# Reading the moving operand of the float32r products in an interleaved column order, with blocks of 496 and 512 columns

## The chip, the cores and the metric

The kernel runs on one core of a Trainium2 chip. The metric is the device time of one execution in microseconds. Before the change it is 2344.78 us, the median of 3 runs (2344.65 to 2344.81).

## The reference

Attention over channels, followed by two feed-forward layers, for B = 2 batches of N = 6016 tokens with C = 256 channels:

```
qn = q / (norm(q, axis=1) + 1e-6);  kn = k / (norm(k, axis=1) + 1e-6)
s  = kn.transpose(0, 2, 1) @ qn / tau            # 256 x 256 per batch
a  = softmax(s)                                  # by rows
x  = (v @ a).reshape(B * N, C)
h  = x @ w_in;   g = h - tanh(h);   x = g @ w_out        # 256 -> 2048 -> 256
out = (sigmoid(x @ w_gate) * (x @ w_val)) @ w_out2       # 256 -> 1536 -> 256
```

## The kernel before

A first stage reads q and k of batch 0, forms the 256x256 scores and their softmax, and multiplies the softmax into w_in (`aw_chunk`, L285), so that h comes straight from v: `aw = a @ w_in`. The same for batch 1 runs in the background, between the blocks' products.

The tokens are then taken in 24 blocks, 12 for each batch, of 500, 504 or 512 tokens (`blocks`, L55 to L70: ten of 500, one of 512 and one of 504 in each batch). Tokens are columns: v and out lie in memory as channels by tokens, and each tile of a block has 128 partitions and one column per token. A block goes through four products, each in 128x128 stationary tiles of weights with the block's columns as the moving operand:

- H (`emit_H`, L324 and L326): h = aw^T v, 16 tiles f of 128 features.
- `emit_E` (L334 to L342): g = h - tanh(h) on ScalarE (ACT) and VectorE (DVE).
- X (`emit_X`, L370, L371, L373): x2 = w_out^T g, summed over the 16 tiles f into two PSUM tiles.
- GV (`emit_GV`, L405, L406, L408): gate and value of x2, 12 tiles m; `emit_S` multiplies sigmoid(gate) by value.
- O (`emit_O`, L437): out = w_out2^T p, summed over m into two PSUM tiles; `emit_out` copies and stores them.

Every float32 operand is split into a high part, rounded to float32r, and the low rest, also float32r. A product is then three: high by high, high by low, low by high. So H has 6 matmuls for each f, X 6 for each f, GV 12 for each m and O 6 for each m. That is 96 + 96 + 144 + 72 = 408 matmuls per block. For block 0, and the first 4 tiles f of block 1 (`XF`), X is done in plain float32 (L365) from one unsplit operand instead. A plain float32 product is issued as two matmul instructions, as are the scores of the first stage (L562, L509).

The order of the work is written out by hand: one loop over steps T with 16 steps per block. In a step stand E of tile f-1, the split and X of tile f-2, H of tile f, and GV and O of some tile m of the block before, which the tables `GV0`, `OFF1`, `OFFS` and `OFFL` place. TensorE (PE) runs it in that order. H and GV write into four rotating PSUM tiles (`psw`), so PE cannot run further ahead than ACT and DVE empty these.

Of the kernel before, what the change touches and what calls it, by code (L numbers as in the profile page):

```python
# [26 lines left out]
def kernel(  # L27
# [14 lines left out]
    B, N, C = q.shape  # L42
# [7 lines left out]
    TB = 4 * P  # L50
    MM = nc.tensor.matmul
    NW = 64


    WB = 500  # L55
    nb = -(-N // TB)
    widths = [WB] * nb
    rest, i = N - WB * nb, nb // 2
    assert 0 <= rest <= nb * (TB - WB)
    while rest:  # L60
        x = min(rest, TB - WB)
        widths[i] += x
        rest -= x
        i = (i + 1) % nb
    blocks = []
    for b in range(B):
        t = 0
# [29 lines left out]
    def psw(name, shape=(P, 512)):  # L97
        return ps_w.tile(list(shape), F32, tag="w", name=name)
# [12 lines left out]
    aw_hi = [wp.tile([P, NK, 2 * P], F32R, name=f"awh{i}") for i in range(N1 // 2)]  # L111

    win = [wp.tile([P, NK, 2 * P], F32, tag=f"awl{i}", name=f"win{i}") for i in range(N1 // 2)]
    aw_lo = {}
# [188 lines left out]
    def split_v(p):  # L303
# [8 lines left out]
            out=lo[:, :, :n], in0=vt, in1=h[:, :, :n].bitcast(F32), op=ALU.subtract  # L312
        )

    hps, g_t, ghl = {}, {}, {}

    def emit_H(p, f):
        n = blocks[p][2]
        h, lo = vT[p]
        o = psw(f"h{p}_{f}")  # L320
        i, fs = f // 2, slice((f % 2) * P, (f % 2 + 1) * P)
        for x in (h, lo):
            for kk in range(2):
                MM(o[:, :n], aw_hi[i][:, kk, fs], x[:, kk, :n], start=x is h and kk == 0, stop=False)  # L324
        for kk in range(2):
            MM(o[:, :n], aw_lo[i][:, kk, fs], h[:, kk, :n], start=False, stop=kk == 1)  # L326
        hps[p, f] = o

    def emit_E(p, f):
# [26 lines left out]
    def emit_X(p, f):  # L356
        n = blocks[p][2]
        if f == 0:
            xps[p] = [ps_x.tile([P, 512], F32, tag=f"x{d}", name=f"x{d}_{p}") for d in range(2)]
        i, a = f // 2, f % 2  # L360
        ds = [slice(d * P, (d + 1) * P) for d in range(2)]
        if p == 0 or p == 1 and f < XF:
            g = g_t.pop((p, f))
            for d in range(2):
                MM(xps[p][d][:, :n], w1_f[i][:, a, ds[d]], g, start=f == 0, stop=f == N1 - 1)  # L365
            return
        gh, gl = ghl.pop((p, f))
        for d in range(2):
            o = xps[p][d][:, :n]
            MM(o, w1_hi[i][:, a, ds[d]], gh, start=f == 0, stop=False)  # L370
            MM(o, w1_lo[i][:, a, ds[d]], gh, start=False, stop=False)  # L371
        for d in range(2):
            MM(xps[p][d][:, :n], w1_hi[i][:, a, ds[d]], gl, start=False, stop=f == N1 - 1)  # L373

    x2 = {}
# [19 lines left out]
    gvps, p_t, phl = {}, {}, {}  # L395

    def emit_GV(p, m):
        n = blocks[p][2]
        h, lo = x2[p]
        ms = slice((m % 2) * P, (m % 2 + 1) * P)  # L400
        res = []
        for nm, wht, wlt in (("ga", wg_hi, wg_lo), ("va", wv_hi, wv_lo)):
            o = psw(f"{nm}{p}_{m}")
            for d in range(2):
                MM(o[:, :n], wht[m // 2][:, d, ms], h[d][:, :n], start=d == 0, stop=False)  # L405
                MM(o[:, :n], wlt[m // 2][:, d, ms], h[d][:, :n], start=False, stop=False)  # L406
            for d in range(2):
                MM(o[:, :n], wht[m // 2][:, d, ms], lo[d][:, :n], start=False, stop=d == 1)  # L408
            res.append(o[:, :n])
        gvps[p, m] = res  # L410

# [13 lines left out]
    def emit_O(p, m):  # L425
        n = blocks[p][2]
        if m == 0:
            ops[p] = [ps_o.tile([P, TB], F32, tag=f"o{d}", name=f"o{d}_{p}") for d in range(NK)]
        ph, pl = phl.pop((p, m))
        i, a = m // 2, m % 2  # L430
        ds = [slice(d * P, (d + 1) * P) for d in range(NK)]
        last = p == NB - 1 and m == N2 - 1
        for d, w, x in ((0, w2_hi, ph), (0, w2_lo, ph), (1, w2_hi, ph), *(
            ((0, w2_hi, pl), (1, w2_lo, ph), (1, w2_hi, pl)) if last else
            ((1, w2_lo, ph), (0, w2_hi, pl), (1, w2_hi, pl))
        )):
            MM(ops[p][d][:, :n], w[i][:, a, ds[d]], x, start=m == 0 and w is w2_hi and x is ph,  # L437
               stop=m == N2 - 1 and x is pl)
# [35 lines left out]
    while len(e_of) < NT:  # L474
        for home in ("x2h", "x2l", *(f"rr{i}" for i in range(6))):
            j = len(e_of)
            n = min(2 if home[0] == "x" else 1, NT - j)
# [52 lines left out]
    ms = tc.manual_schedule()  # L530
# [182 lines left out]
    for n in range(3 * N2 // 2):  # L713
        i, w = divmod(n, 3)
# [3 lines left out]
    for j in range(NT):  # L718
        t = 54 + 2 * j
# [36 lines left out]
    for T in range(-4, (NB + 1) * N1 + 18):  # L756
# [14 lines left out]
        for u in mg:  # L771
            emit_GV(*u)
# [3 lines left out]
        if e0 and first:  # L776
            emit_H(*e0)
# [7 lines left out]
        if e2:  # L785
            emit_X(*e2)
            if e2[1] == N1 - 1:
                emit_x2(e2[0])
        for u in mo:
            emit_O(*u)  # L790
# [9 lines left out]
        if e0 and not first:  # L800
            emit_H(*e0)
# [39 lines left out]
```

## Time and profile before

| | |
|---|---|
| time, median of 3 runs | 2344.78 us |
| span of the profiled execution | 2342.6 us |
| PE busy | 2330.5 us (99%) |
| PE weight loads busy | 1932.8 us (83%) |
| DVE busy | 1799.2 us (77%) |
| ACT busy | 1575.5 us (67%) |
| granted TensorE clock | 1.00 from 5 us to the end |

The profiled execution's span is 2.2 us below the median time, since launch and end of the program lie outside it. A busy time is the union of an engine's instructions. The duration of a matmul in the profile reaches from its first column to its modelled end, so consecutive matmuls overlap: what one costs PE is the distance between two starts, not its duration.

### The profile page before, as it was taken

The page shows a single profiled execution, that of the slowest core. Times are in us where ns is not written, and L with a number is a line of the kernel's source. Part 1 is how long each engine was busy: PE and PEld are TensorE (multiplying, and loading weights), DVE is VectorE, ACT ScalarE, POOL GpSimd, SP SyncE. Part 2 cuts the span into 40 slices and gives each one's busy share as a digit, 9 for nine tenths or more (in the row PEclk, how much of TensorE's full clock was granted, in tenths as well). Part 3 has the DMA queues.
Part 4 walks back from the last instruction along what each step waited for, and adds up shares of the span by engine and source line. Part 5 has one row for each costly group of instructions (what it writes and reads, how often), then busy time and mean ns, then how long its engine had stood idle before and what let it go on. Part 6 is the DMA issues. An engine that isn't in the chain of part 4 may idle for free.

```text
span 2342.6 us, 28855 instructions
## 1 busy us (share of the span) xinstructions
PE 2330.5 (99%) x10338; PEld 1932.8 (83%) x10338; DVE 1799.2 (77%) x2791; ACT 1575.5 (67%) x2777; POOL 67.2 (3%) x53
## 2 busy tenths in 40 slices
PE   9999999999999999999999999999999999999999
PEld 7778788888888888888888888888888888888887
DVE  7999877787878777777777777777777777777773
ACT  6677666776767667766676666666666666666663
POOL 0000000111111110000000000000000000000000
PEclk9999999999999999999999999999999999999999
DMA  9742001101101100000000000000000000000000
GB/s 353 225 132 90 27 1 50 33 26 50 32 28 45 32 27 18 1 23 32 18 18 14 6 18 1 18 18 1 18 18 1 18 18 1 18 1 18 10 1 18
DMA packets 54000, 86.54 MB, mean 37 GB/s; under 512 B 4960, under 2 KB 34144, under 8 KB 53856
## 3 DMA queue, kind: packets, MB, share of 16 engines
q1 hardware_dynamic: 53280, 83.91, 11.1%
q8 instruction: 81, 1.33, 0.2%
q10 hardware_dynamic: 576, 0.79, 0.1%
q14 instruction: 63, 0.52, 0.1%
HBM read 69.73 MB, written 14.94 MB: 36 GB/s over the span
## 4 chain that ended last, share of the span: by engine, by line
PE 90%; DVE 7%; ACT 1%; issue 1%; DMA 0%; ACTq 0%; DVEq 0%; SPq 0%
PE o L437 16%; PE h L324 14%; PE h L326 7%; PE x L373 7%; PE x L370 7%; PE x L371 7%; PE ga L405 5%; PE ga L406 5%; PE va L405 5%; PE va L406 5%; PE ga L408 5%; PE va L408 5%; DVE accb L573 1%; DVE w L341 1%; DVE w L342 1%
## 5 line engine op out<-in xcount | busy, mean ns | idle before, releaser
L339 DVE SCALAR_TENSOR_TENSOR w<-u,h 128x500 f32<-128x500 f32 (+2 forms) x384 | 259.3, 675 | 327.0 <-ACT t L335 326.8
L334 ACT ACTIVATE u<-h 128x500 f32<-128x500 f32 (+2 forms) x384 | 223.7, 583 | 248.0 <-PE h L326 245.5
L342 DVE COPY_PREDICATED w<-m,t 128x500 f32<-128x500 uint16 (+2 forms) x384 | 306.2, 797 | 39.9 <-ACT sr L679 0.5
L337 ACT ACTIVATE s<-u,cb 128x500 f32<-128x500 f32 (+2 forms) x384 | 274.5, 715 | 0.7 <-DVE w L341 0.6
L338 ACT ACTIVATE m<-u,ct 128x500 bf16<-128x500 f32 (+2 forms) x384 | 272.8, 710 | 0.0
L340 DVE TENSOR_TENSOR t<-h,t 128x500 f32<-128x500 f32 (+2 forms) x384 | 258.2, 672 | 0.0
L341 DVE SCALAR_TENSOR_TENSOR w<-s,w 128x500 f32<-128x500 f32 (+2 forms) x384 | 257.3, 670 | 0.0
L324 PE MATMUL h<-vTh,awh 128*128 128x500 f32 (+2 forms) x768 | 243.9, 399 | 0.0
L324 PE MATMUL h<-vTl,awh 128*128 128x500 f32 (+2 forms) x768 | 235.4, 387 | 0.9 <-DVE vTl L311 0.9
L326 PE MATMUL h<-vTh,awl 128*128 128x500 f32 (+2 forms) x768 | 235.5, 388 | 0.0
L335 ACT ACTIVATE t<-h 128x500 f32<-128x500 f32 (+2 forms) x384 | 223.6, 582 | 1.7 <-PE x L365 1.0
L405 PE MATMUL ga<-x2h,wgh 128*128 128x500 f32 (+2 forms) x552 | 213.6, 387 | 0.0
L406 PE MATMUL va<-x2h,wvl 128*128 128x500 f32 (+2 forms) x552 | 213.6, 387 | 0.0
L406 PE MATMUL ga<-x2h,wgl 128*128 128x500 f32 (+2 forms) x552 | 213.6, 387 | 0.0
L405 PE MATMUL va<-x2h,wvh 128*128 128x500 f32 (+2 forms) x552 | 213.4, 387 | 0.0
L417 DVE TENSOR_TENSOR sg<-va,sg 128x500 f32<-128x500 f32 (+2 forms) x288 | 192.3, 668 | 20.9 <-PE va L408 20.9
L416 ACT ACTIVATE sg<-ga 128x500 f32<-128x500 f32 (+2 forms) x288 | 169.2, 587 | 15.7 <-PE ga L408 12.8
L408 PE MATMUL ga<-x2l,wgh 128*128 128x500 f32 (+2 forms) x576 | 176.1, 387 | 0.0
L408 PE MATMUL va<-x2l,wvh 128*128 128x500 f32 (+2 forms) x576 | 176.0, 387 | 0.0
L324 PEld LDWEIGHTS h<-vTh,awh 128*128 128x128 f32 x768 | 143.6, 188 | 34.5 <-issue 7.1
L324 PEld LDWEIGHTS h<-vTl,awh 128*128 128x128 f32 x768 | 144.4, 188 | 30.6 <-DVE vTl L311 1.4
L326 PEld LDWEIGHTS h<-vTh,awl 128*128 128x128 f32 x768 | 144.2, 188 | 28.9
(361 smaller groups left out, 4449.8 us busy)
## 6 DMA issues: line engine op xcount, KB each, us to landing
v<-in_v_dram SPq DMA_DIRECT2D x20, 500.0 KB, 4.2
out_dram<-ob SPq DMA_DIRECT2D x19, 500.0 KB, 3.2
sr<-in_q_dram SPq DMA_DIRECT2D x47, 128.0 KB, 2.1
sr<-in_k_dram SPq DMA_DIRECT2D x47, 128.0 KB, 2.2
raw<-in_q_dram SPq DMA_DIRECT2D x13, 384.0 KB, 8.1
raw<-in_k_dram SPq DMA_DIRECT2D x12, 384.0 KB, 8.2
st_wi<-in_moe_w_in_dram SPq DMA_DIRECT2D x8, 512.0 KB, 7.0
st_w<-in_moe_w_out_dram SPq DMA_DIRECT2D x8, 512.0 KB, 4.8
```

What stands on the lines that cost most here:

```text
L324: MM(o[:, :n], aw_hi[i][:, kk, fs], x[:, kk, :n], start=x is h and kk == 0, stop=False)
L326: MM(o[:, :n], aw_lo[i][:, kk, fs], h[:, kk, :n], start=False, stop=kk == 1)
L337: nc.scalar.activation(s, u, AF.Square, bias=cb)
L338: nc.scalar.activation(m, u, AF.Relu, bias=ct2)
L339: nc.vector.scalar_tensor_tensor(out=w, in0=u, scalar=C2, in1=hp, op0=ALU.mult, op1=ALU.mult)
L340: nc.vector.tensor_tensor(out=t, in0=hp, in1=t, op=ALU.subtract)
L341: nc.vector.scalar_tensor_tensor(out=w, in0=s, scalar=CG, in1=w, op0=ALU.add, op1=ALU.mult)
L342: nc.vector.copy_predicated(w, m.bitcast(U16), t)
L405: MM(o[:, :n], wht[m // 2][:, d, ms], h[d][:, :n], start=d == 0, stop=False)
L406: MM(o[:, :n], wlt[m // 2][:, d, ms], h[d][:, :n], start=False, stop=False)
L408: MM(o[:, :n], wht[m // 2][:, d, ms], lo[d][:, :n], start=False, stop=d == 1)
L437: MM(ops[p][d][:, :n], w[i][:, a, ds[d]], x, start=m == 0 and w is w2_hi and x is ph, stop=m == N2 - 1 and x is pl)
```

## The change

Three things change; the sequence of instructions on every engine and queue stays the same, one for one.

1. Each moving operand of H, X, GV and O in float32r is read through a view, `turned`, that takes the columns of each group of 16 in the order 0, 8, 1, 9, 2, 10, and so on to 7, 15. For blocks 0 and 1 (`PB = 2`) the group is 8 columns and the order is 0, 4, 1, 5, 2, 6, 3, 7. The output is written in plain order, so each product permutes the block's columns. Four such products in a row give back the first order for groups of 16, and three do for groups of 8; in blocks 0 and 1 X is read plainly, so there H, GV and O are the three.
2. The widths of the blocks must be multiples of 16. In each batch they become eight of 496 and four of 512 columns. The number of blocks, of matmuls and of columns in all is as before.
3. ACT and DVE read and write their tiles plainly, as before, in the new widths.

```
-    WB = 500
+    QB = 16
+    assert N % QB == 0
     nb = -(-N // TB)
+    WB = N // nb // QB * QB
     widths = [WB] * nb
     rest, i = N - WB * nb, nb // 2
     while rest:
-        x = min(rest, TB - WB)
-        widths[i] += x
-        rest -= x
+        widths[i] += QB
+        rest -= QB
         i = (i + 1) % nb
...
+    PB = 2
+
+    def turned(p, x):
+        return x.rearrange("p (a t i) -> p a i t", t=2, i=4 if p < PB else QB // 2)
...
-                MM(o[:, :n], aw_hi[i][:, kk, fs], x[:, kk, :n], start=x is h and kk == 0, stop=False)
+                MM(o[:, :n], aw_hi[i][:, kk, fs], turned(p, x[:, kk, :n]), start=x is h and kk == 0, stop=False)
...
-        gh, gl = ghl.pop((p, f))
+        gh, gl = (x if p < PB else turned(p, x) for x in ghl.pop((p, f)))
...
-        h, lo = x2[p]
+        h, lo = ([turned(p, x[:, :n]) for x in y] for y in x2[p])
...
-        ph, pl = phl.pop((p, m))
+        ph, pl = (turned(p, x) for x in phl.pop((p, m)))
```

## Rows read from the trace of the kernel before

**Rows 1.** The page, busy time (share of the span) and instructions by engine

```profile
PE 2330.5 (99%) x10338; PEld 1932.8 (83%) x10338; DVE 1799.2 (77%) x2791; ACT 1575.5 (67%) x2777; POOL 67.2 (3%) x53
PEclk9999999999999999999999999999999999999999
```

**Rows 2.** Waits, total us, times, longest: PE's two longest, then DVE's and ACT's

```profile
PE kq L562 <- DMA raw<-in_k_dram: 2.5, 2, 1.4
PE va L406 <- DVE wvl L150: 1.3, 1, 1.3
...
DVE w L339 <- ACT t L335: 326.8, 322, 3.4
ACT u L334 <- PE h L326: 245.5, 177, 3.1
```

**Rows 3.** Windows by block; the fourth row is all from block 3 on

```profile
core 0: us, PE busy (x) PEld busy (x) DVE busy (x) ACT busy (x) POOL busy (x), PEclk, DMA share, GB/s
60.50:140.10 79.60, 79.60 (x311) 58.24 (x309) 76.45 (x133) 52.02 (x91) 0.00 (x0) 1.00 0.63 193
140.10:238.30 98.20, 96.46 (x406) 75.66 (x405) 93.86 (x159) 72.14 (x128) 0.00 (x0) 1.00 0.33 105
238.30:339.70 101.40, 99.51 (x440) 82.12 (x438) 77.53 (x125) 66.11 (x119) 0.00 (x0) 1.00 0.05 16
339.70:2338.70 1999.00, 1998.73 (x8927) 1668.66 (x8925) 1502.80 (x2309) 1347.97 (x2398) 65.23 (x46) 1.00 0.06 19
523.40:615.30 91.90, 91.90 (x410) 76.69 (x409) 73.60 (x108) 64.99 (x117) 11.39 (x9) 1.00 0.12 35
1364.40:1455.50 91.10, 91.10 (x409) 76.60 (x408) 68.48 (x108) 61.40 (x110) 0.00 (x0) 1.00 0.04 12
1728.90:1821.20 92.30, 92.30 (x409) 76.59 (x408) 69.28 (x108) 62.12 (x110) 0.00 (x0) 1.00 0.04 12
1821.20:1915.10 93.90, 93.90 (x409) 76.69 (x408) 69.34 (x108) 62.27 (x110) 0.00 (x0) 1.00 0.04 12
2099.30:2191.20 91.90, 91.90 (x409) 76.70 (x408) 68.52 (x108) 61.53 (x110) 0.00 (x0) 1.00 0.04 12
```

**Rows 4.** Chain that ended last: start us, us, products; L509 plain float32, L285 float32r

```profile
143.21 1.73 PE kqe L509 x8
...
1102.71 1.41 PE aw L285 x12
```

**Rows 5.** Single lines: durations ns min/median/max; win plain float32, wh float32r; loads PEld

```profile
L365 PE MATMUL x<-w,w1f x80: 582/582/687, 70.8 to 169.8; 128*128 128x500 f32 x80
...
L285 PE MATMUL aw<-win,aT x64: 378/379/382, 57.2 to 120.8; 128*128 128x256 f32 x64
L285 PEld LDWEIGHTS aw<-wh,aTh x32: 187/188/188, 1102.3 to 1187.7; 128*128 128x128 f32 x32
L285 PE MATMUL aw<-wh,aTh x32: 277/280/282, 1102.6 to 1187.8; 128*128 128x256 f32 x32
```

**Rows 6.** Groups on PE by shape: count, busy us, mean ns of one

```profile
L326 PE MATMUL h<-vTh,awl 128*128 128x500 f32 x640 | 196.0, 387 | 0.0
...
L406 PE MATMUL ga<-x2h,wgl 128*128 128x500 f32 x456 | 175.8, 386 | 0.0
```

**Rows 7.** Timeline of PE: 12 products of X and H, then 18 of O and GV

```profile
1002.58 0.39 PE L370 MATMUL x<-g_1h,w1h 128*128 128x500 f32 x1
...
1005.30 0.39 PE L405 MATMUL ga<-x2h,wgh 128*128 128x500 f32 x1
...
2331.33 0.39 PE L437 MATMUL o<-p_9h,w2h 128*128 128x500 f32 x1
...
2335.35 0.39 PE L437 MATMUL o<-p_10h,w2h 128*128 128x500 f32 x1
```

**Rows 8.** Window of those last 18 products, columns as in Rows 3

```profile
2331.33:2335.35 4.02, 4.02 (x19) 3.38 (x18) 1.36 (x2) 1.21 (x2) 0.00 (x0) 1.00 0.00 0
```

More of the change, by code (lines that the diff above doesn't have):

```diff
@@ L323, in emit_H @@
             for kk in range(2):
-                MM(o[:, :n], aw_hi[i][:, kk, fs], x[:, kk, :n], start=x is h and kk == 0, stop=False)
+                MM(o[:, :n], aw_hi[i][:, kk, fs], turned(p, x[:, kk, :n]), start=x is h and kk == 0, stop=False)
         for kk in range(2):
-            MM(o[:, :n], aw_lo[i][:, kk, fs], h[:, kk, :n], start=False, stop=kk == 1)
+            MM(o[:, :n], aw_lo[i][:, kk, fs], turned(p, h[:, kk, :n]), start=False, stop=kk == 1)
         hps[p, f] = o
@@ L404, in emit_GV @@
             for d in range(2):
-                MM(o[:, :n], wht[m // 2][:, d, ms], h[d][:, :n], start=d == 0, stop=False)
-                MM(o[:, :n], wlt[m // 2][:, d, ms], h[d][:, :n], start=False, stop=False)
+                MM(o[:, :n], wht[m // 2][:, d, ms], h[d], start=d == 0, stop=False)
+                MM(o[:, :n], wlt[m // 2][:, d, ms], h[d], start=False, stop=False)
             for d in range(2):
-                MM(o[:, :n], wht[m // 2][:, d, ms], lo[d][:, :n], start=False, stop=d == 1)
+                MM(o[:, :n], wht[m // 2][:, d, ms], lo[d], start=False, stop=d == 1)
             res.append(o[:, :n])
```

## Prediction

> **What bounds the kernel now.** I read the page first. PE is busy 99% of the span, at full granted clock throughout [rows 1]. The waits say the same: PE's two longest add up to 3.8 us, while DVE waits 326.8 us for ACT's tanh and ACT 245.5 us for PE's h [rows 2]. The windows then show where this does not hold: DVE is busy 96% of the first two blocks (76.45 of 79.6 us, 93.86 of 98.2). From block 3 on it is busy 75%, and PE has no gap worth naming (1998.73 of 1999.0 us) [rows 3]. So a faster matmul shortens the last 1999 us almost one for one, and the 180 us ahead of block 2 hardly.
>
> Busy, though, is not the same as at its peak, so the next question is what one product costs. Plain float32 gives the scale: 582 ns for 500 columns and 379 ns for 256 [rows 5], so 203 ns for 244 columns, 0.832 ns each. [...] Eight instructions of 256 columns start within 1.73 us [rows 4], 216.3 ns each, of which 512 cycles are 213.3. The fixed part is 2.9 ns.
>
> Float32r takes one pass, so a column should cost 0.417 ns. The durations say 386 to 387 ns for 500 columns [rows 6] against 280 for 256 [rows 5]: 106.5 ns for 244 columns, 0.436 each, or 1.05 cycles. Starts say the same. Twelve products of 256 columns take 1.41 us [rows 4], 117.5 ns each, against 106.7 + 2.9 = 109.6: 7.9 ns too much. The long window gives the price of the blocks' products. Of its 8925 weight loads [rows 3], 96 belong to `aw` and 16 to the second softmax. The remaining 8813 are H and X of 21 blocks, GV and O of 22, and 29 that trail from the block before. The window less 96 x 0.1175 and about 1.6 us for the 16 is 1986.1 us, which makes 225.4 ns per product. At the mean width, 6016 / 12 = 501.33 columns, one cycle per column and the fixed part make 208.9 + 2.9 = 211.8 ns. **So 13.5 ns, or 32 cycles, are lost in every product, about one cycle in 16 columns.** With 256 columns 19 are lost, so the loss grows with the columns and is no fixed cost.
>
> Where does it come from? Not from the other engines: the 18 products from 2331.33 to 2335.35 [rows 7] take 223.3 ns each while DVE is busy 1.36 of 4.02 us and ACT 1.21 [rows 8], and a block at 91.1 us also comes to 223.3 (91.1 / 408) with DVE busy 75% [rows 3]. Not from the weight loads' length: they last 188 ns, and with 256 columns they follow each other every 117.5 ns [rows 4, 5]. Nor is it a fixed rate. At equal shape 12 products of X and H take 2.72 us, 226.7 ns each, and 18 of O and GV 223.3 [rows 7]; blocks of one shape and one mix take 91.1 or 91.9 us; and the block with H of 504 columns beside O of 512 takes 93.9, though H of 512 beside O of 500 needs only 92.3 [rows 3], where the columns (207,360 against 206,304) explain 0.4 of the 1.6 us. A loss that differs among equal products depends on which words are read when. That is why I think the order of reading can change it.
>
> **The change part by part.** The instructions stay the same one for one, so no queue is moved and no wait is added; only addresses and widths differ.
>
> *The order.* No row shows a float32r matmul that reads columns 8 apart, so I bound it. Below: the whole loss goes, 13.5 ns for each of 8813 products, 119 us. Above: each column needs two cycles, as plain float32's columns do, which is the nearest row in which PE reads 4-byte columns more slowly: 1000 cycles for 500 columns and the fixed part, 416.7 + 2.9 = 420 ns, against 211.8. I take the first end, since the loss is small and varies with position, more like a collision between neighbouring reads than a limit of the path: a limit would cost equal products equally. Term: -119 us.
>
> *Blocks 0 to 2 ahead of that window.* Of about 9600 changed products (24 x 408 less 16 x 6 + 4 x 6 = 120 of X, and 72 more of block 1's X that read plainly) 787 lie before 339.7 us, worth 10.6 us at most. DVE's 96% allows little in the first two blocks. I take about half: -5 us; the ends are 0 and -10.6.
>
> *The widths.* Columns in all and instructions in all stay the same, so ACT's and DVE's work stays the same as well. At a price that is linear in the columns, PE's does too: 0.
>
> *What is late next.* A 500-column block shrinks by 408 x 13.5 = 5.5 us, from 91.9 to 86.4. In the fullest stretch DVE has 73.60 us of work in it and ACT 64.99 [rows 3], so 85% and 75%. Neither becomes the bound, but E's chain from h to g has less room. The nearest row with PE waiting on it is block 2, where PE idles 1.89 of 101.4 us at a DVE share of 76%. Over 21 blocks that would be 40 us, the upper end. PE's waits now are near zero at 80%, so I take +3 us. Weight loads of 188 ns still fit into 211.8.
>
> Sum: -119 - 5 + 3 = -121 us against the profiled execution, whose span of 2342.6 lies 2.2 us below the median; the difference carries over, so 2344.8 - 121 = **2224 us**. Its own range is 2208 (both earlier terms whole, no new wait, and the fixed part 0.7 ns smaller, which is what the two digits of 1.73 us leave open) to 2250 (a sixth of the loss stays).
>
> **The rivals.**
>
> *Slower: the turned order costs a change of place at every column.* The plain order reads neighbours; the new one jumps 32 bytes at each column (16 in blocks 0 and 1). If the reader gets several neighbouring words at once, it throws away all but one each time. The decision lies at 13.5 ns: up to 32 lost cycles in 500 columns nothing is lost against now, beyond that it is slower. One cycle more in 16 than now gives 9600 x 13.5 = +130 us, 2474; two cycles per column, as in plain float32, give 9600 x (420 - 225.4) = +1.87 ms, 4210 us. For it: the plain order, with neighbours, comes within 6% of the ideal. Against it: the loss in that order shows that neighbours are not free either.
> [...]
>
> *The order changes nothing.* Then only the widths act. Blocks of 512 would cost between 91.5 x 512 / 500 = 93.7 us and 92.3 + (93.9 - 91.5) = 94.7; blocks of 496 between 91.1 x 496 / 500 = 90.4 and 91.5 [rows 3]. For 24 blocks, 16 of 496 and 8 of 512, that is 2196 to 2222, against 20 x 91.5 + 2 x (92.3 + 93.9) = 2202 now: -6 to +19 us, so 2339 to 2364, the middle 2351. For it: the loss could belong to the rate and not to the place. Against it: the differences among equal products.
>
> *Part of it is given back*, by a loss that only halves (2224 + 60 = 2284) or by PE waiting for E as in block 2 (2224 + 37 = 2261): 2250 to 2335.
>
> **How the numbers follow.** Chances: 0.60 for the forecast, 0.12 for part of it, 0.12 for no effect of the order, 0.16 for slower. About 0.2%, 4.7 us, is what a measurement of this kernel can tell from no change. Faster by more: 0.60 + 0.12 = 0.72. Within it (2340.1 to 2349.5): half of the third case, 0.06. Slower: its other half and the last, 0.22. The range must leave out no more than 2 in 10. The slower rival is 0.16, so it reaches from 2208 across the third case's middle to 2355, and holds about 0.79. Faster cases alone hold 0.72 of it; the likeliest's own range is 2208 to 2250.
>
> **What the changed profile would show.** If right: matmuls of 496 columns last about 12 ns less than now at equal columns (582 ns less 1000 cycles leave 166 ns beside the columns, so 379 for 512 and 372 to 373 for 496), start every 209.6 ns, a block of 496 takes about 85.5 us, H and X cost what GV and O do, PE stays at 99% and DVE rises to about 81%. If the jumps cost more than the neighbours, durations grow, towards 580 ns at the worst, and ACT and DVE wait longer. If the order does nothing, starts stay 222 to 233 ns apart. If E is late, PE shows waits for h's PSUM tiles in blocks 3 to 9. The forecast is wrong if starts in a steady block stay over 214 ns apart.

## The result and the profile after

The changed kernel takes 2219.34 us (median of 4 runs, 2218.63 to 2220.04) against 2344.8 us: a ratio of 0.9465, 95% interval 0.9452 to 0.9478. The forecast was 2224 us.

The windows of the changed kernel by block, with columns as in [rows 3]: blocks 0, 1, 2, all from block 3 on, a block with background work, one of 496 columns and one of 512.

```profile
60.60:140.00 79.40, 78.38 (x311) 58.11 (x309) 76.25 (x133) 51.86 (x91) 0.00 (x0) 1.00 0.60 191
140.00:235.90 95.90, 92.41 (x406) 75.72 (x405) 93.19 (x159) 71.52 (x127) 0.00 (x0) 1.00 0.34 107
235.90:331.00 95.10, 92.51 (x439) 82.54 (x439) 76.77 (x125) 65.21 (x118) 0.00 (x0) 1.00 0.05 17
331.00:2213.00 1882.00, 1880.87 (x8927) 1677.93 (x8925) 1501.21 (x2311) 1337.53 (x2398) 64.71 (x46) 1.00 0.06 20
502.10:587.80 85.70, 85.60 (x410) 77.02 (x409) 72.83 (x108) 64.21 (x118) 11.15 (x8) 1.00 0.12 38
1296.50:1381.80 85.30, 85.30 (x409) 77.09 (x408) 67.96 (x108) 60.38 (x109) 0.00 (x0) 1.00 0.04 13
1812.30:1900.40 88.10, 88.10 (x410) 77.13 (x409) 69.51 (x108) 61.94 (x109) 0.00 (x0) 1.00 0.04 13
```

The window from block 3 on shrinks from 1999.0 us [rows 3] to 1882.0, by 117.0, with the same 8925 weight loads. Blocks 0 to 2 shrink from 279.2 to 270.4 us, by 8.8. Together that is the whole difference of the spans, 2342.6 - 2216.8 = 125.8. A block of 496 columns takes 85.3 us for 408 products, 209.1 ns each; one of 512 takes 88.1, 215.9 ns: 6.8 ns for 16 columns, 0.42 each. At the prediction's 0.417 ns per column, half of plain float32's 0.832 [rows 5], the columns make 206.7 and 213.3 ns, so 2.4 to 2.6 ns are left beside them. The loss of about 13.5 ns per product is gone.

The groups on PE by shape (count, busy us, mean ns of one) answer to [rows 6], and two rows of the timeline to [rows 7]:

```profile
L335 PE MATMUL h<-vTh,awl 128*128 128x496 f32 x512 | 149.1, 373 | 0.4 <-DVE awl L292 0.4
L415 PE MATMUL ga<-x2h,wgl 128*128 128x496 f32 x360 | 134.1, 372 | 0.0
L335 PE MATMUL h<-vTh,awl 128*128 128x512 f32 x256 | 76.1, 379 | 0.0
```

```profile
1301.50 0.37 PE L446 MATMUL o<-p_10h,w2h 128*128 128x496 f32 x1
...
1304.01 0.37 PE L379 MATMUL x<-g_0h,w1h 128*128 128x496 f32 x1
```

Durations are 372 to 373 ns for 496 columns and 379 for 512, which is also what plain float32 takes for 256 columns [rows 5]. Six products of O and six of H start within 2.51 us, 209.2 ns each: products that cost 223.3 and 226.7 ns [rows 7] now cost the same. The waits say that PE is still the bound, with less room around it:

```profile
PE va L415 <- DVE wvl L151: 1.5, 1, 1.5
...
PE x L382 <- DVE g_13l L357: 0.8, 1, 0.8
...
DVE w L348 <- ACT t L344: 220.5, 305, 3.0
ACT u L343 <- PE h L335: 140.3, 131, 2.7
```

DVE's wait for ACT's tanh and ACT's wait for PE's h, the longest of each, are 106.3 and 105.2 us shorter than before [rows 2]. PE's longest single wait is 1.5 us.

### The profile page after: what moved, and what is told of

Its sections match the earlier page's. It is cut to its first block, busy times and chain, and to the rows that moved or that the text cites. A ratio compares the mean times of both kernels' runs of the same rounds, so it can differ in the third digit from the quotient of the medians.

```text
span 2216.8 us, 28854 instructions
## 1 busy us (share of the span) xinstructions
PE 2201.8 (99%) x10338; PEld 1943.3 (88%) x10338; DVE 1796.0 (81%) x2791; ACT 1563.4 (71%) x2777; POOL 66.7 (3%) x53
## 4 chain that ended last, share of the span: by engine, by line
PE 87%; DVE 7%; ACT 2%; DMA 1%; issue 1%; DVEq 0%; SPq 0%
PE o L446 15%; PE h L333 13%; PE x L382 7%; PE h L335 7%; PE x L379 6%; PE x L380 6%; PE ga L417 5%; PE ga L415 5%; PE ga L414 5%; PE va L417 5%; PE va L415 5%; PE va L414 5%; DVE w L351 1%; DVE w L350 1%; PE kq L571 1%
## 5 line engine op out<-in xcount | busy, mean ns | idle before, releaser
L348 DVE SCALAR_TENSOR_TENSOR w<-u,h 128x496 f32<-128x496 f32 (+1 forms) x384 | 259.6, 676 | 221.3 <-ACT t L344 220.5
L351 DVE COPY_PREDICATED w<-m,t 128x496 f32<-128x496 uint16 (+1 forms) x384 | 302.8, 789 | 40.6 <-DVE w L350 1.4
L346 ACT ACTIVATE s<-u,cb 128x496 f32<-128x496 f32 (+1 forms) x384 | 273.8, 713 | 2.5 <-DVE w L350 2.5
L347 ACT ACTIVATE m<-u,ct 128x496 bf16<-128x496 f32 (+1 forms) x384 | 272.5, 710 | 0.0
L349 DVE TENSOR_TENSOR t<-h,t 128x496 f32<-128x496 f32 (+1 forms) x384 | 258.5, 673 | 0.0
L350 DVE SCALAR_TENSOR_TENSOR w<-s,w 128x496 f32<-128x496 f32 (+1 forms) x384 | 257.7, 671 | 0.0
L333 PE MATMUL h<-vTh,awh 128*128 128x496 f32 (+1 forms) x768 | 232.9, 385 | 0.0
L333 PE MATMUL h<-vTl,awh 128*128 128x496 f32 (+1 forms) x768 | 225.1, 375 | 1.0 <-DVE vTl L312 1.0
L335 PE MATMUL h<-vTh,awl 128*128 128x496 f32 (+1 forms) x768 | 225.2, 375 | 0.4 <-DVE awl L292 0.4
L344 ACT ACTIVATE t<-h 128x496 f32<-128x496 f32 (+1 forms) x384 | 223.2, 581 | 2.1 <-DVE w L348 1.7
```

The costliest lines, as they stand in the source:

```text
L333: MM(o[:, :n], aw_hi[i][:, kk, fs], turned(p, x[:, kk, :n]), start=x is h and kk == 0, stop=False)
L335: MM(o[:, :n], aw_lo[i][:, kk, fs], turned(p, h[:, kk, :n]), start=False, stop=kk == 1)
L346: nc.scalar.activation(s, u, AF.Square, bias=cb)
L347: nc.scalar.activation(m, u, AF.Relu, bias=ct2)
L348: nc.vector.scalar_tensor_tensor(out=w, in0=u, scalar=C2, in1=hp, op0=ALU.mult, op1=ALU.mult)
L349: nc.vector.tensor_tensor(out=t, in0=hp, in1=t, op=ALU.subtract)
```

## The experiments

The theory was that the loss belongs to the order in which neighbouring 4-byte columns are read, whatever the widths, the distance of the jump and the other engines. The rivals: the widths in multiples of 16 made the gain; only short jumps are free; any order that avoids neighbours will do; the weight load that runs beside each product collides with the moving read. In the expectations a line is 16 bytes, four float32r columns, counted from a tile's first column. It is the author's unit for these tests; what the runs show of it is prices: 227 ns at distance 2 and 215.8 at distance 4 (m1), 226 from a start two columns on and 215.8 from four (m2).

### Widths alone (e1_widths)

```
-        return x.rearrange("p (a t i) -> p a i t", t=2, i=4 if p < PB else QB // 2)
+        return x
```

> The changed widths (496 and 512) with the plain order everywhere. Theory (the order alone brings the gain): 2339 to 2364 us, no more than 0.3% under the kernel before; products of 496 start 221 to 226 ns apart. Rival (multiples of 16 columns end the loss, the order does nothing): 2219 us, starts at 209 ns.

It took 2346.67 us, a ratio of 1.0006 (0.9997 to 1.0015): no change that can be measured. The windows of a block of 496 columns and of one of 512:

```profile
1364.80:1455.30 90.50, 90.50 (x410) 76.61 (x409) 68.06 (x108) 61.06 (x110) 0.00 (x0) 1.00 0.04 12
1913.30:2007.50 94.20, 94.20 (x409) 76.62 (x408) 69.71 (x108) 62.36 (x110) 0.00 (x0) 1.00 0.04 12
```

Products still cost 221.8 and 230.9 ns (90.5 and 94.2 us by 408). The order makes the whole gain.

### The order alone, with far jumps (e2_order_oldw)

The widths of before, and the two halves of the block read in turn:

```
-    WB = N // nb // QB * QB
+    WB = 500
...
-        widths[i] += QB
-        rest -= QB
+        x = min(rest, TB - WB)
+        widths[i] += x
+        rest -= x
...
-        return x.rearrange("p (a t i) -> p a i t", t=2, i=4 if p < PB else QB // 2)
+        return x.rearrange("p (t i) -> p i t", t=2)
```

> The widths of before (500, 504, 512), with each moving operand read from its two halves in turn: columns 0, n/2, 1, n/2 + 1 and so on, a jump of about 1000 bytes at each column. The four products no longer give back the first order, so within a block the output's tokens stand in another order. Theory (any jump out of the 16-byte line ends the loss): 2219 us within 5, products of 500 start 210.8 ns apart. Rival (only jumps within 64 bytes are free, or the widths matter): 2340 us or more; in between if far jumps cost part of it.

It took 2220.26 us, a ratio of 0.9467 (0.9453 to 0.9482). A block of 500 columns took 86.0 us, 210.8 ns per product, in place of 91.1 to 91.9 [rows 3]:

```profile
1384.70:1470.70 86.00, 86.00 (x409) 77.11 (x408) 68.42 (x108) 60.70 (x109) 0.00 (x0) 1.00 0.04 13
```

So neither the widths nor a short jump is needed. The groups of 16 and the widths only serve to give back the tokens' order.

### GV alone (e3_gv_only)

```
-                MM(o[:, :n], aw_hi[i][:, kk, fs], turned(p, x[:, kk, :n]), start=x is h and kk == 0, stop=False)
+                MM(o[:, :n], aw_hi[i][:, kk, fs], x[:, kk, :n], start=x is h and kk == 0, stop=False)
...
-        gh, gl = (x if p < PB else turned(p, x) for x in ghl.pop((p, f)))
+        gh, gl = ghl.pop((p, f))
...
-        ph, pl = (turned(p, x) for x in phl.pop((p, m)))
+        ph, pl = phl.pop((p, m))
```

> The changed widths, with the turned order in GV's 3456 products alone; H, X and O read plainly, so the tokens of a block stand in another order in the output. In the run with plain order throughout GV's products of 496 and 512 columns started about 223.3 and 233.2 ns apart, in the changed kernel 209.2 and 215.8: 14.1 and 17.4 ns less, a mean of 15.2. Theory (each product pays for itself, PE is the bound): 2346.7 - 3456 x 15.2 = 2294 us within 4. Rival (the gain needs neighbouring products of the same order, or other engines give it back): 2310 us or more.

It took 2297.14 us, a ratio of 0.9793 (0.9777 to 0.981), 49.5 us less than widths alone: 14.3 ns for each of 3456 products, where 15.2 were expected, and 3 us more than the 2294 forecast, inside its margin of 4. Means of one product on PE, H plain and GV turned in the same run:

```profile
L335 PE MATMUL h<-vTh,awl 128*128 128x496 f32 x512 | 154.9, 383 | 0.0
L415 PE MATMUL ga<-x2h,wgl 128*128 128x496 f32 x360 | 134.0, 372 | 0.0
```

H's products last as long as plain ones and GV's as in the changed kernel: each product pays for itself, whatever order its neighbours have.

### A turn inside 16 bytes (e4_dist2)

```
-        return x.rearrange("p (a t i) -> p a i t", t=2, i=4 if p < PB else QB // 2)
+        return x.rearrange("p (a t i) -> p a i t", t=2, i=2)
```

> The changed kernel with columns in the order 0, 2, 1, 3 of each four: turned, but inside the 16 bytes of a line. (In blocks 0 and 1 three such products do not give back the first order, so their tokens stand in another order.) Theory (the jump must leave the line): 2335 to 2350 us. Rival (any order that is not neighbour by neighbour is enough): 2219 us.

It took 2346.97 us, a ratio of 1.0008 (0.9999 to 1.0017), as with the plain order. GV's products of 496 columns last 384 to 387 ns, against 372 in the changed kernel. A turn inside four columns gains nothing.

### Bare products in many orders (m1_orders)

Series of 36 products of 512 columns beside changing 128x128 weights, with nothing else at work; one of the series:

```
probe("turnc", turn(x[:, :512], 8), 512)   # columns 0, 8, 1, 9, ... of each 16
```

> This kernel leaves out the whole computation: it runs series of 36 products on TensorE alone, one reading order of the moving operand per series, and stores zeros. No other engine works beside it. Free spacing is 512 / 2.4 + 2.4 = 215.7 ns (the changed kernel's 512-column products start 215 to 216 ns apart); the kernel before showed about 13 to 17 ns more. Theory (the loss belongs to reading neighbouring 4-byte columns one after the other): plain float32r 512 starts 228 to 233 ns apart here too, with no other engine at work; a jump out of the 16-byte line at each column (orders with distances 4, 8, 16, 32, 128, 256) gives 216; bf16 plain gives 216; plain float32, two cycles per column, 429 in either order. Rival 1 (the change of place as such costs, and only distances within 64 bytes are cheap): distances 4 and 8 give 216, 16 and more give clearly over 229. Rival 2 (the loss comes from collisions of the weight load with the moving read): weights read with a step of two columns change the plain spacing. Rival 3 (any order that is not neighbour by neighbour is enough): distance 2, which stays inside 16 bytes, gives 216 as well; by the theory in its narrow form it keeps 228 or so. Pairs, quads and octets of neighbours taken in turn from the two halves tell how long a run of neighbours may be: by the theory pairs are free and octets show the loss.

PE's timeline merges each series into one row (start us, us, count); the distance between two series' starts, divided by 36, is the price of a product. DVE waits 308.7 us for the last series and ACT's last copy begins at 13.1 us, so both are idle beside the series; from 29.76 to 45.90 and from 62.16 to 66.40 us the granted clock is 1.00. offa begins 4 columns later than the first series. turna to turng have distances of 2, 4, 8, 16, 32, 128 and 256 columns. pairs, quads and octs take 2, 4 and 8 neighbours at a time from the two halves, four takes columns 4 apart in turn from each 16, stepb, stepd and steph read every 2nd, 4th and 8th column. wstep is plain order beside weights that are read with a step of two columns. bplain and bturn are bfloat16, the latter at distance 8; fplain and fturn are plain float32, 12 products in 24 instructions.

```profile
70.45 8.55 PE L52 MATMUL offa<-xr,wr 128*128 128x512 f32 x36
78.84 8.56 PE L52 MATMUL offb<-xr,wr 128*128 128x512 f32 x36
87.24 8.35 PE L52 MATMUL turna<-xr,wr 128*128 128x512 f32 x36
95.42 7.93 PE L52 MATMUL turnb<-xr,wr 128*128 128x512 f32 x36
103.19 7.93 PE L52 MATMUL turnc<-xr,wr 128*128 128x512 f32 x36
...
142.04 12.40 PE L52 MATMUL pairs<-xr,wr 128*128 128x512 f32 x36
154.27 9.18 PE L52 MATMUL quads<-xr,wr 128*128 128x512 f32 x36
163.29 8.92 PE L52 MATMUL octs<-xr,wr 128*128 128x512 f32 x36
172.05 9.82 PE L52 MATMUL four<-xr,wr 128*128 128x512 f32 x36
181.71 16.48 PE L52 MATMUL stepb<-xr,wr 128*128 128x512 f32 x36
198.01 16.78 PE L52 MATMUL stepd<-xr,wr 128*128 128x512 f32 x36
...
230.14 8.58 PE L52 MATMUL wstep<-xr,wr 128*128 128x512 f32 x36
238.56 7.94 PE L52 MATMUL bplain<-xb,wb 128*128 128x512 bf16 x36
246.34 17.64 PE L52 MATMUL bturn<-xb,wb 128*128 128x512 bf16 x36
263.82 17.50 PE L52 MATMUL bturng<-xb,wb 128*128 128x512 bf16 x36
281.16 10.46 PE L52 MATMUL fplain<-raw 128*128 128x512 f32 x24
291.46 13.01 PE L52 MATMUL fturn<-raw 128*128 128x512 f32 x24
```

Plain float32r loses here too (offa 8.39 us by 36, 233 ns), so the other engines have no part in it. Distance 2 costs 227 ns; distances 4 (7.77 us by 36) to 256 all cost 215.8. Plain bfloat16 costs 216. So far as expected. Not expected: pairs cost 340 ns, quads 251, octs 243 and four 268, all more than plain order, though pairs and quads were to be free. With a step of 2 it is 453. In bfloat16 the same turn that helps float32r costs 486 ns in place of 216. In plain float32, at 429 ns for an instruction in plain order, the series of 24 lasts 13.01 us in place of 10.46, 106 ns more for each, though either order was to cost 429. The sign of the weight rival appeared too: wstep costs 234 ns (8.42 us by 36), while plain order from the same columns costs 227 (pa below). The narrow theory, that it is neighbour after neighbour that costs, fell with the pairs.

### Two streams (m2_streams)

The new theory was a guess from these prices: the columns at the even and those at the odd places of the order are two streams, and a product is free where each stream takes several columns from one line before it leaves it (a visit). Plain order gives each two per visit, distance 8 four, pairs one.

```
probe("db", turn(x[:, :504], 6), 504)
probe("reptwo", <each pair of 256 columns read twice>, 512)
```

> This kernel too leaves out the whole computation: series of 36 products on TensorE alone. Theory (two streams: the columns at even places of the order and those at odd places are read apart, and a stream is free while it takes four columns from each 16-byte line before it leaves it; plain order gives each stream two): distances 12 and 36 (multiples of four columns) start 504 / 2.4 + 2.4 = 212.4 ns apart; distance 6 (runs of four and of two) and a start one or two columns off a line lose part, 213 to 227; distance 3 (runs of one and two) loses more than plain order, over 223; each column read twice in a row (repone), each pair twice (reptwo) and each four twice (repfour), 256 columns for 512 places, give every stream four reads of a line and are free, 215.8; six columns 4 apart in turn change the line at each read of a stream and cost over 240. Rival (the loss is the price of a neighbour following its neighbour): reptwo and repfour lose as plain order does, 227; distances 3 and 6 are free, 212; starts off a line make no difference. Plain order from nine starts tells whether the place of the first column alone moves the loss between 226 and 234 ns.

pa, pb and pc are plain order from columns 0, 1 and 2; tb, tc, td distance 8 from columns 1, 2, 4; da, db, dc distances 3, 6, 12.

```profile
29.74 8.32 PE L52 MATMUL pa<-xr,wr 128*128 128x512 f32 x36
37.90 8.68 PE L52 MATMUL pb<-xr,wr 128*128 128x512 f32 x36
46.41 8.55 PE L52 MATMUL pc<-xr,wr 128*128 128x512 f32 x36
...
104.57 8.58 PE L52 MATMUL tb<-xr,wr 128*128 128x512 f32 x36
112.99 8.32 PE L52 MATMUL tc<-xr,wr 128*128 128x512 f32 x36
121.14 7.93 PE L52 MATMUL td<-xr,wr 128*128 128x512 f32 x36
...
144.45 9.76 PE L52 MATMUL da<-xr,wr 128*128 128x504 f32 x36
154.04 7.82 PE L52 MATMUL db<-xr,wr 128*128 128x504 f32 x36
161.70 7.81 PE L52 MATMUL dc<-xr,wr 128*128 128x504 f32 x36
...
184.77 7.93 PE L52 MATMUL reptwo<-xr,wr 128*128 128x512 f32 x36
192.54 7.93 PE L52 MATMUL repfour<-xr,wr 128*128 128x512 f32 x36
200.31 10.56 PE L52 MATMUL six<-xr,wr 128*128 128x504 f32 x36
210.70 8.36 PE L52 MATMUL plainz<-xr,wr 128*128 128x512 f32 x36
```

reptwo and repfour cost 215.8 ns although neighbours follow each other in them: the rival is out. Distance 3 costs 266 and six 289, as the streams would have it. The turned order costs 234 from a start one column on and 226 from two, and 215.8 from four: **its gain depends on where the first column lies.** (tb was to end at 227 and did not.) Distance 6, with visits of four and of two, was to lose part and is free: 212.8, against 212.5 at distance 12. Plain order from nine starts costs 227 to 236 ns, so place alone does move the loss.

### Weights and short visits (m3_weights)

```
probe("md", x[:, :512], 512, w=lambda i: wr[:, i, :32])   # weights of 32 columns
probe("gb", turn(x[:, 2:514], 16), 512)                    # distance 16, two columns off a line
```

> A third series of bare products of 512 (504, 500) columns on TensorE alone; nothing of the computation is done. Question 1: does the weight load that runs beside a product cause the loss of the plain order? Theory (no: the two streams of the moving operand do): plain order beside weights of 128, 96, 64 and 32 columns starts 226 to 237 ns apart all the same, and the turned order beside 32 columns 215.8. Rival (the loads' reads collide with the moving reads): the loss of 11 ns shrinks with the columns of the weights, to some 3 ns (218 to 219) at 32. Weights that begin 1 to 64 columns later, or are the same tile each time, tell whether the place of the weights moves the loss between 226 and 237. Question 2: how long must a stream stay in a 16-byte line? Theory, as the runs so far have it (free at a mean of 3 reads per visit, lossy at 2.7): distance 10, distance 6 from two columns off a line, distances 12, 16 and 32 from two columns off (means 3.3, 3.0, 3.0, 3.2, 3.6) are free, 212 to 216; distance 5 (2.5) loses, over 215. Rival (short visits one after the other lose, whatever the mean): distances 12, 16 and 32 from two columns off lose, the less the longer the distance.

ma and md are plain order beside 128 and 32 columns of weights, me the turned order beside 32; wa and wb plain order beside weights one and two columns later; ga, gb, gc distances 12, 16, 32 from column 2, gd distance 16 from column 1, tb distance 5.

```profile
55.09 8.50 PE L53 MATMUL md<-xr,wr 128*32 128x512 f32 x36
63.43 7.93 PE L53 MATMUL me<-xr,wr 128*32 128x512 f32 x36
71.20 8.53 PE L53 MATMUL wa<-xr,wr 128*128 128x512 f32 x36
...
129.42 8.08 PE L53 MATMUL ga<-xr,wr 128*128 128x504 f32 x36
137.34 8.24 PE L53 MATMUL gb<-xr,wr 128*128 128x512 f32 x36
145.42 8.13 PE L53 MATMUL gc<-xr,wr 128*128 128x512 f32 x36
153.39 8.32 PE L53 MATMUL gd<-xr,wr 128*128 128x512 f32 x36
...
195.07 8.69 PE L53 MATMUL tb<-xr,wr 128*128 128x500 f32 x36
203.60 8.35 PE L53 MATMUL plainz<-xr,wr 128*128 128x512 f32 x36
```

Beside a quarter of the weights' columns the plain order costs 232 ns, not less than ma's 227 (8.16 us by 36): the loss does not shrink with the columns of the weights. The place of the weights shifts it (wa 232.5), as their step did in wstep. Since no series runs without loads, it is not shown that the loss needs none of them; the turned order costs 215.8 beside either load. Distances 12, 16 and 32 from column 2 cost 220, 224 and 221, not the free 212 to 216. Distance 10 was free (211 ns for 500 columns) and distance 5 cost 237, as expected. Distance 6 from column 2 was free too (212.5 ns for 504), as expected, but from column 1, for which nothing was forecast, it cost 286 (10.30 us by 36). A mean of three columns per visit is still not the condition; the three orders lose, as the rival said, though not always less at longer distance.

## Why the prediction was right, point by point

- **PE is the bound, its products lose 13.5 ns each, and the order ends the loss.** Held: 117.0 us in the window from block 3 on, where 119 less 3 for new waits were forecast. e1, e2 and e3 show that the order does it, alone and product by product.
- **The free price** was put at 211.8 ns with a fixed part of 2.9. Its cycle is 0.417 ns, half of plain float32's 0.832 for a column [rows 5], and its whole term rests on one such cycle per float32r column. No run shows how many cycles a column takes; what the runs show is the price, 209.1 ns for 496 columns and 215.9 for 512, 0.42 for each column more. At 0.417 the fixed part is 2.4 (209.1 for 496 columns). That is 0.5 ns by 8813, or 4 us, too little gain. What kept the window's 117.0 us near the forecast all the same is in part a shift that the prediction put at nothing: blocks 0 to 2 became four columns narrower each, and the 21 later blocks 12 columns wider together. Twelve columns by 408 products at 0.417 ns, an estimate of at most 2 us, moved into the window; in the whole time it cancels.
- **Blocks 0 to 2: 5 us.** They gave 8.8 of the 10.6 that were the bound: 0.2 in block 0, 2.3 in block 1 and 6.3 in block 2. DVE's share (96 and 97%) bounded the first two, as said: PE's idle time there rose from 1.7 to 4.5 us, so part of what its products gained became waiting. Up to 2 us of the 8.8 are the narrower blocks; taking half for all three was too little for block 2, where PE had been busy 98%.
- **New waits: 3 us.** In the block with background work 85.7 us stand against 85.3 without. Some six such blocks make 2 to 3 us, an estimate from these two rows. In the block shown the wait can be seen: the product at 510.21 us is followed after 0.47 us, in place of 0.21, by the first that reads g_0l. The wait for h's PSUM tiles that was feared does not stand among PE's longest; those behind E are for the split of g.
- **The widths cost nothing.** Held: 1.0006 (0.9997 to 1.0015). The rival's 2339 to 2364 for this case held too, with 90.5 and 94.2 us for the blocks (90.4 to 91.5 and 93.7 to 94.7 were its bounds).
- **The range.** Its inner end of 2250 was called a sixth of the loss; a sixth of 119 us gives 2244, and 2250 leaves about a fifth. Nothing hangs on it.
- **The argument from place was right in result and only partly in mechanism.** The variation among equal products did mean that what is read when decides. But that neighbouring reads collide is not what the runs show: neighbours are free in repfour, and pairs in turn from two halves are worse. Counting by streams and lines fits the sign of most orders (distance 2, 4 to 256, 3, pairs, reptwo, six, tb). It does not give the sizes: plain order, octs and quads have the same two columns per visit or nearly and cost 227, 243 and 251. The streams are the author's guess from prices; no run shows how the columns are read. The prediction chose the whole loss as its term because a collision of neighbours seemed likelier than a dear jump; four (268), six (289) and distance 5 (237) part neighbours as well and cost more than plain order, so it was in part luck that the chosen order ends the whole loss.
- **The slower rival** fails for this order and holds for others. Every second column costs 453 ns and every fourth 461 (16.61 us by 36, from 198.01 to 214.62). Four columns, 16 bytes, mark a step, with distance 2 at 227 and distance 4 at 215.8. But a column from another line at each place of the order is dear in one order and free in another: 461 ns with every fourth column, 215.8 where two lines are taken in turn, less than plain order with its four neighbours per line (227). Every second column, two from each line, costs 453.

Left open: what makes plain order's price range from 227 to 236 ns with the starts of the moving tile and of the weights, what part the weight loads have in it, why distance 6 is free from column 2 and not from column 1, and why bfloat16 and plain float32 lose by the turn that helps float32r.

## What to carry to other kernels

A product in float32r whose moving operand is read plainly cost some 5 to 10% more here than it need (227 to 236 ns against 215.8 for 512). Where such products bound a kernel, read the columns from two places in turn. From a tile's first column distances 4, 6, 8, 10, 12, 16, 32, 36, 128 and 256 were free (215.8 ns for 512 columns, 211 to 213 for 500 and 504), and 250 in e2 (210.8 for 500); 2, 3 and 5 were not (227, 266 and 237), though 5 columns are 20 bytes. At distance 8 starts one and two columns on were not free (234 and 226), a start four on was. Choose a permutation that a chain of products undoes. Not so with bfloat16 or plain float32, which lost by it (486 ns in place of 216, and 106 more for each instruction), and not by reading with a step, which cost 453 ns at 2 columns and 461 at 4.

## What had not been expected of the hardware

Bfloat16 columns read in turn 16 bytes apart cost 486 ns for 512, 2.25 times the plain order's 216; every second float32r column costs 453 ns, more than the 429 of a plain float32 instruction. A far jump is as cheap as a near one: 1 KB at each column costs 215.8 ns.
